# Slots-first relu and two-head turn of q, three output tiles side by side, first denominators by halves

## The chip, the core and the metric

The kernel runs on one core of one Trainium2 chip. The metric is the device time of one execution in microseconds (us), the median of several executions. All executions told of here are of the fast state (granted TensorE clock 0.997 to 1.0), apart from four single looks at the kernel before. The kernel before took 325.89 us (median of 6 runs, 325.66 to 326.36).

## The reference, cut to what matters

Linear attention with a cosine feature map (8 batches, 8 heads, 576 positions, head size 64) feeds a gated feed-forward block (4608 tokens, 512 wide, 1536 hidden). Only relu is applied to q before it is weighted with cosine and sine of the position.

```python
def phi(x, c, s):
    r = np.maximum(x, 0.0)
    return np.concatenate([r * c, r * s], axis=-1)
q_p, k_p = phi(q, cos_w, sin_w), phi(k, cos_w, sin_w)
kv  = np.einsum('bhsf,bhsd->bhfd', k_p, v);   z = np.sum(k_p, axis=2)
den = np.einsum('bhsf,bhf->bhs', q_p, z)[..., None] + 1e-06
x   = np.einsum('bhsf,bhfd->bhsd', q_p, kv) / den      # -> [4608, 512]
...
g   = x @ w_gate
out = (g * (1.0 / (1.0 + np.exp(-g))) * (x @ w_val)) @ w_out
```

## The kernel before

The work goes by groups of 512 tokens. For each group TensorE makes twelve blocks f=0 to 11 of gate and value products (L503, with `wg_sb` and `wv_sb`), ScalarE the silu `sg`, VectorE the product `ht`, and TensorE then the output products with `wo_sb` (L539). While the first group runs, the attention for the next batch has to be made ready in between: q is turned (transposed) by TensorE so that positions become columns, kv is summed up, and the products of the two (the a-products) follow.

The turn before the change reads q as it was loaded. It transposes one head at a time into half of the partitions, and relu is applied as the result is copied out of PSUM (on ScalarE 0.914 us for 128x896 in this kernel):

```python
def qturn_pe(b, j, lo, hi, eng):
    ps = take(1).bitcast(BF16).rearrange("p (c x) -> p c x", x=P)
    for c in range(lo, hi):
        for i in range(2):
            nc.tensor.transpose(out=ps[i * D:(i + 1) * D, c - lo], in_=raws[b, "q"][:, 2 * j + i, c],
                                identity=ident)
    relu_op(eng, qt_of(b)[:, :, j, lo:hi].rearrange("p e c s -> p c e s"),
            ps[:, 0:hi - lo].rearrange("p c (e s) -> p c e s", e=2))
```

Such turns come three times: one slot of q of batch one during block 9, seven slots of batch two after block 11 ("the large turn"), and the last two slots of batch two during the output products ("the second turn"). The order of the start and of blocks 0 to 5 (the first 28.75 us) is written out as a list of words, executed one by one; blocks 6 to 11 run by halves of 256 columns; the output tiles of the first group run two side by side:

```python
words = """
    cq0@act cq1@act tq0 qr0@dve qw0.0 qw0.1 rk1.0@act rk0.0@dve z8 kv0.0 rk3.0@dve rk2.0@dve kv1.0
    ...
""".split()                       # cq cast q, tq turn q, qr relu, qw weight, rk relu k, kv products, z filler products of zeros
...
for g, s in enumerate(("a10", "a11", "b8", "b9")):
    at(s, lambda g=g: vmul(1, g))                 # the four v products on VectorE
at("b11", q_(1, 0, 0), q_(1, 1, 0), lambda: kv_mm(1), lambda: kv_out(1))
...
for nm, f in order:                               # halves a6 a7 b6 b7 a8 ...
    ffn_fc(0, f, *((HALF, GH) if nm == "b" else (0, HALF)))
    slot(f"{nm}{f}")
steps0 = [(piece, t) for piece in range(3) for t in range(2)] + [(piece, t) for t in (2, 3) for piece in range(3)]
for i, (piece, t) in enumerate(steps0):
    ffn_out(t, 4 * piece, 4 * piece + 4)          # a third of wo for one tile of 128 tokens
    slot(divmod(i, 4))
```

## Time and profile before

| stretch of TensorE's stream (profiled run, 326.35 us) | from | to | us |
|---|---|---|---|
| start, until the first gate product | 0 | 16.41 | 16.41 |
| blocks 0 to 5 | 16.41 | 28.75 | 12.34 |
| blocks 6 to 11 | 28.75 | 39.66 | 10.91 |
| large turn, kv, output products, second turn | 39.66 | 55.49 | 15.83 |
| second group to the last product | 55.49 | 320.51 | 265.03 |

Two of these stretches as the view by stretches of time has them. Its columns are the length, then the busy us (and instructions) of TensorE, its weight loads, VectorE, ScalarE and GpSimd, then the granted clock, and two figures for the DMAs (share and GB/s) that are not used here:

```profile
28.75:39.66 10.91, 10.91 (x103) 9.34 (x100) 8.15 (x19) 4.97 (x15) 5.19 (x7) 1.00 1.30 204
39.66:55.49 15.83, 15.83 (x194) 9.12 (x194) 10.28 (x29) 10.23 (x21) 0.00 (x0) 1.00 1.22 222
```

TensorE is busy for the whole of both. The timeline of TensorE around the large turn (start, length, what ran; an idle time would stand in brackets at the end) shows that nothing is waited for there:

```profile
39.13 0.60 PE L503 MATMUL banks<-xT,wv_sb 128*128 128x256 bf16 x4
39.66 0.97 PE L264 MATMUL banks<-ident,raw_q 128*64 128x128 bf16 x28
40.56 1.24 PE L276 MATMUL banks<-v,raw_k 64*64 64x130 bf16 x72
```

The reader should see `128*64` against `128*128`: a turn to half of the partitions is listed with another shape than the products around it. Four products of 256 columns start 0.437 us apart as a block, so the transposes could have begun at 39.57 and began at 39.66: 0.09 us pass at this change of shape.

### The profile page before, as it was taken

What the parts mean: (1) busy time and instruction counts of PE and PEld (TensorE: products, weight loads), DVE (VectorE), ACT (ScalarE), POOL (GpSimd) and SP (SyncE); (2) the same over time, 40 slices, a digit from 0 to 9 for tenths busy, and PEclk for the clock granted to TensorE, in tenths of its full rate; (3) what the DMA queues carried; (4) which work ended last, traced back from release to release, by engine and by line L of the source; (5) the groups of instructions that cost most, each with busy time, mean ns of one, the idle gap of its engine ahead of it and who ended that gap; (6) DMA issues with size and microseconds to landing.
All of it is one profiled execution on the core that took longest, in us unless ns stands there. A gap on an engine that the chain in (4) does not pass through costs nothing.

```text
span 324.6 us, 6212 instructions
## 1 busy us (share of the span) xinstructions
PE 318.0 (98%) x2474; PEld 164.6 (51%) x2474; DVE 181.8 (56%) x366; ACT 132.3 (41%) x247; POOL 34.8 (11%) x58
## 2 busy tenths in 40 slices
PE   7999999999999999999999999999999999999995
PEld 3589855454545444544454445444554445444443
DVE  7775866976575647565657555755564236423420
ACT  7553565943653335332642354344432132213311
POOL 6755200002002000110002000200000000000000
PEclk9999999999999999999999999999999999999999
DMA  7999999499676997699689969794921411240014
GB/s 264 215 199 199 205 205 221 70 125 149 147 125 80 185 153 128 93 170 163 120 111 140 164 129 130 119 186 110 134 46 34 106 26 32 44 103 17 2 32 97
DMA packets 71660, 40.37 MB, mean 124 GB/s; under 512 B 47184, under 2 KB 66384, under 8 KB 71632
## 3 DMA queue, kind: packets, MB, share of 16 engines
q1 hardware_dynamic: 49280, 22.29, 37.9%
q0 software_dynamic: 22192, 17.57, 35.5%
q8 instruction: 19, 0.31, 0.4%
q10 hardware_dynamic: 160, 0.13, 0.1%
q14 instruction: 9, 0.07, 0.1%
HBM read 37.75 MB, written 9.44 MB: 145 GB/s over the span
## 4 chain that ended last, share of the span: by engine, by line
PE 95%; DMA 2%; DVE 1%; ACT 0%; SPq 0%; issue 0%; ACTq 0%
PE banks L503 58%; PE banks L539 28%; PE banks L276 3%; PE banks L390 2%; DMA first_q<-in_q_dram 2%; PE banks L475 1%; PE banks L434 1%; PE banks L149 1%; PE banks L558 1%; PE banks L264 0%; PE banks L316 0%; PE banks L372 0%; SPq L117 0%; DVE qwT L360 0%; ACT ob L561 0%; ACT qf L339 0%
## 5 line engine op out<-in xcount | busy, mean ns | idle before, releaser
L514 DVE TENSOR_TENSOR ht<-sg,banks 128x512 bf16<-128x512 bf16 (+2 forms) x122 | 75.8, 625 | 68.1 <-PE banks L503 62.3
L509 ACT ACTIVATE sg<-banks 128x512 bf16<-128x512 f32 (+2 forms) x122 | 66.9, 548 | 113.6 <-PE banks L503 109.0
L503 PE MATMUL banks<-xT,wv_sb 128*128 128x512 bf16 (+2 forms) x488 | 112.8, 355 | 0.1
L503 PE MATMUL banks<-xT,wg_sb 128*128 128x512 bf16 (+2 forms) x488 | 112.6, 355 | 0.0
L539 PE MATMUL banks<-wo_sb,ht 128*128 128x512 bf16 x420 | 94.3, 379 | 0.0
L503 PEld LDWEIGHTS <-wv_sb 128*128 128x128 bf16 x488 | 47.2, 98 | 46.7 <-issue 0.4
L503 PEld LDWEIGHTS <-wg_sb 128*128 128x128 bf16 x488 | 45.7, 98 | 41.6
L539 PEld LDWEIGHTS <-ht 128*128 128x128 bf16 x420 | 40.1, 98 | 45.2 <-issue 0.2
L546 ACT COPY ob<-banks 128x512 f32<-128x512 f32 x18 | 10.5, 585 | 51.2 <-PE banks L539 49.2
L232 DVE TENSOR_TENSOR r_q<-raw_q,tab 128x1152 bf16<-128x1152 bf16 x24 | 17.9, 754 | 20.2 <-ACT raw_q L215 20.2
L546 DVE COPY ob<-banks 128x512 f32<-128x512 f32 x17 | 11.8, 691 | 28.9 <-PE banks L539 28.0
L236 DVE TENSOR_TENSOR v<-raw_v,tab 128x1152 bf16<-128x1152 bf16 x31 | 23.0, 752 | 0.3 <-ACT raw_v L570 0.3
L411 DVE TENSOR_TENSOR x<-banks,rec 128x512 bf16<-128x512 f32 (+1 forms) x32 | 21.5, 674 | 1.1
L714 POOL COPY hold<-phit 1x2 bf16<-1x2 bf16 x5 | 0.9, 176 | 155.1 <-DMA phit<-r_q 155.1
L215 ACT ACTIVATE raw_q<-raw_q 128x576 bf16<-128x576 bf16 x24 | 15.7, 680 | 0.8 <-DMA raw_q<-in_q_dram 0.8
L215 ACT ACTIVATE raw_k<-raw_k 128x576 bf16<-128x576 bf16 x24 | 16.0, 675 | 0.0
L390 PEld LDWEIGHTS <-phit 128*128 128x128 bf16 (+1 forms) x240 | 9.9, 100 | 6.0 <-issue 1.3
L390 PE MATMUL banks<-kv,phit 128*128 128x65 bf16 (+1 forms) x240 | 11.5, 195 | 0.0
L149 PE MATMUL banks<-zeros 128*128 128x64 bf16 (+1 forms) x66 | 8.7, 290 | 1.0 <-DVE zeros L144 1.0
L299 DVE CAST kv<-banks 64x260 bf16<-64x260 f32 x12 | 5.1, 428 | 7.4 <-ACT kv L299 7.4
L276 PEld LDWEIGHTS <-raw_k 64*64 64x64 bf16 x504 | 7.5, 106 | 2.6 <-issue 2.1
L276 PE MATMUL banks<-v,raw_k 64*64 64x130 bf16 x504 | 8.7, 218 | 0.0
(79 smaller groups left out, 134.3 us busy)
## 6 DMA issues: line engine op xcount, KB each, us to landing
out_dram<-ob SPq DMA_DIRECT2D x70, 128.0 KB, 2.4
raw_k<-in_k_dram POOLq DMA_DIRECT2D x7, 576.0 KB, 9.6
raw_q<-in_q_dram POOLq DMA_DIRECT2D x6, 576.0 KB, 6.1
raw_v<-in_v_dram POOLq DMA_DIRECT2D x6, 576.0 KB, 12.3
wo_sb<-in_moe_w_out_dram POOLq DMA_DIRECT2D x3, 512.0 KB, 12.7
wg_sb<-in_moe_w_gate_dram POOLq DMA_DIRECT2D x5, 256.0 KB, 9.0
wv_sb<-in_moe_w_val_dram POOLq DMA_DIRECT2D x5, 256.0 KB, 9.2
wo_sb<-in_v_dram SPq DMA_DIRECT2D x2, 576.0 KB, 4.1
```

The costliest lines, as they stand in the source:

```text
L149: nc.tensor.matmul(out=ps, lhsT=zeros, rhs=zeros[:, 0:cols].unsqueeze(1).to_broadcast([P, 4, cols]), start=True, stop=True)
L215: nc.scalar.activation(out=out, in_=in_, func=AF.Relu)
L232: nc.vector.tensor_tensor(out=st[b, "q"][:, g], in0=o.unsqueeze(2).to_broadcast([P, NC, 2, D]), in1=tab, op=ALU.mult)
L236: nc.vector.tensor_tensor(out=v2s[b % 2][:, g, :, :, 0:D], in0=(first if b == 0 and g == 0 else {"v": raw_of(b, "v")})["v"][:, g].unsqueez ...
L276: nc.tensor.matmul(out=ps[i * D:(i + 1) * D, e, j * 2 * D1:(j + 1) * 2 * D1], lhsT=raws[b, "k"][es, g, c], rhs=v2s[b % 2][es, g, c, :, 0:D ...
L390: nc.tensor.matmul(out=ps[ms, e, g * D1:(g + 1) * D1], lhsT=phit[b][:, e, g, c:c + n].rearrange("p c s -> p (c s)"), rhs=kv2s[b % 2][:, e, ...
L411: nc.vector.tensor_tensor(out=st["x", t].rearrange("p (y e d) -> p e y d", e=2, d=D)[:, :, ys], in0=ps[:, :, 0:2 * J * D1].rearrange("p e ...
L503: nc.tensor.matmul(out=st["f", tg, fc, lo][i], lhsT=(wg_sb, wv_sb)[i][:, kc, fs], rhs=xT[tg][:, ts, kc], start=(kc == 0), stop=(kc == KC - 1))
L509: nc.scalar.activation(out=sg[:, 0:n], in_=st["f", tg, fc, lo][0], func=AF.Silu)
L514: nc.vector.tensor_tensor(out=hts[tg % 2][:, fc, r:r + n], in0=st.pop(("s", tg, fc, lo))[:, 0:n], in1=ps[1], op=ALU.mult)
L539: nc.tensor.matmul(out=o_ps[t], lhsT=hts[tg % 2][:, fc, r:r + P], rhs=wo_sb[:, fc], start=(fc == 0), stop=(fc == FC - 1))
L546: (nc.scalar.copy if t % 2 == 0 else nc.vector.tensor_copy)(out=ob, in_=ps)
```

## The change

The intent has four parts. The first denominators are made by halves, with a new list of words for the start and blocks 0 to 5, so that the first group starts earlier. Blocks 6 to 11 run in 512 columns and not by halves. q is put slots-first by a relu on VectorE into a new tile, so that two heads stand side by side and one transpose turns both; the copy out of PSUM is then plain. And three output tiles of the first group run side by side, which puts off the need for the later thirds of wo. The diff, cut to its core:

```diff
+    def relu_slots(b, lo, hi):
+        if "qp" not in st:
+            both = rel.tile([P, G, NC, 2, D], BF16, name="r_q").rearrange("p g c w d -> p (g c w d)")
+            st["qp"] = both.rearrange("p (b c j x) -> p b c j x", b=2, c=NC, j=J)
+        relu_op("dve", st["qp"][:, b, lo:hi].rearrange("p c j (i d) -> p c (j i) d", i=2),
+                raws[b, "q"][:, :, lo:hi].rearrange("p g c d -> p c g d"))
...
         for c in range(lo, hi):
-            for i in range(2):
-                nc.tensor.transpose(out=ps[i * D:(i + 1) * D, c - lo], in_=raws[b, "q"][:, 2 * j + i, c],
-                                    identity=ident)
-        relu_op(eng, qt_of(b)[:, :, j, lo:hi].rearrange("p e c s -> p c e s"),
+            nc.tensor.transpose(out=ps[:, c - lo], in_=st["qp"][:, b, c, j], identity=ident)
+        copy_op(eng, qt_of(b)[:, :, j, lo:hi].rearrange("p e c s -> p c e s"),
...
-        cq0@act cq1@act tq0 qr0@dve qw0.0 qw0.1 rk1.0@act rk0.0@dve z8 kv0.0 rk3.0@dve rk2.0@dve kv1.0
+        cq1@act cq0@dve tq0 qr0@dve rk0.0@act rk1.0@dve qw0.0 qw0.1 z6 kv0.0 rk2.0@dve rk3.0@dve kv1.0
...
+    at("a8", lambda: relu_slots(0, NC - 1, NC))
...
-    at("a9", lambda: relu_k(1, 2, 4, "dve"))
+    at("a9", lambda: relu_k(1, 2, 4, "act"))
-    for g, s in enumerate(("a10", "a11", "b8", "b9")):
+    for g, s in enumerate(("b9", "b9", "b10", "b10")):
         at(s, lambda g=g: vmul(1, g))
+        if g == 2:
+            at(s, lambda: relu_slots(1, 0, CUT))
...
+    at((0, 3), lambda: relu_slots(1, CUT, NC))
...
-    for nm, f in order:
-        ffn_fc(0, f, *((HALF, GH) if nm == "b" else (0, HALF)))
-        slot(f"{nm}{f}")
+    for f in range(6, FC):
+        ffn_fc(0, f)
...
-    steps0 = [(piece, t) for piece in range(3) for t in range(2)] + [(piece, t) for t in (2, 3) for piece in range(3)]
+    steps0 = [(piece, t) for piece in range(3) for t in range(3)] + [(piece, 3) for piece in range(3)]
```

Also in it: one relu of k moves from VectorE to ScalarE and the v products come later in VectorE's order (both in the cut above), `x_den` and `x_rec` take halves, the pools of x and `sg` get one buffer more each, and the choice of a PSUM bank avoids splitting a free pair.

More of the change, by code (lines that the diff above doesn't have):

```diff
@@ L50 @@
     phip = ctx.enter_context(tc.tile_pool(name="phip", bufs=2))
-    xp = ctx.enter_context(tc.tile_pool(name="xp", bufs=3))
+    xp = ctx.enter_context(tc.tile_pool(name="xp", bufs=4))
     xtp = ctx.enter_context(tc.tile_pool(name="xtp", bufs=3))
     smp = ctx.enter_context(tc.tile_pool(name="smp", bufs=3))
-    sgp = ctx.enter_context(tc.tile_pool(name="sgp", bufs=4))
+    sgp = ctx.enter_context(tc.tile_pool(name="sgp", bufs=5))
     obp = ctx.enter_context(tc.tile_pool(name="obp", bufs=4))
@@ L66, in take @@
     def take(n, hold=None):
-        free = [b for b in range(0, 8, n) if not any(b <= x < b + n for r in held.values() for x in r)]
-        b0 = min(free, key=lambda b: sorted(used[b:b + n], reverse=True))
+        taken = {x for r in held.values() for x in r}
+        free = [b for b in range(0, 8, n) if not any(b <= x < b + n for x in taken)]
+        b0 = min(free, key=lambda b: (n == 1 and hold is not None and hold[0] == "o" and b ^ 1 not in taken,
+                                      sorted(used[b:b + n], reverse=True)))
         if hold is not None:
@@ L395, in a_tile2, with x_den, x_rec @@
         x_of(t, ps)
-    def x_den(t, ps):
-        den = smp.tile([P, H, 1], FP32, name="den")
+    def x_den(t, ps, ys=slice(0, 4)):
+        if ys.start == 0:
+            st["den", t] = smp.tile([P, H, 1], FP32, name="den")
         nc.vector.tensor_single_scalar(
-            out=den.rearrange("p (e y) o -> p e y o", e=2),
-            in_=ps[:, :, 0:2 * J * D1].rearrange("p e (y x) -> p e y x", x=D1)[:, :, :, D:D1], scalar=1e-6, op=ALU.add)
-        st["den", t] = den
-    def x_rec(t):
-        rec = smp.tile([P, H, 1], FP32, name="rec")
-        nc.vector.reciprocal(out=rec, in_=st.pop(("den", t)))
-        st["rec", t] = rec
-        st["x", t] = xp.tile([P, d_model], BF16, name="x")
+            out=st["den", t].rearrange("p (e y) o -> p e y o", e=2)[:, :, ys],
+            in_=ps[:, :, 0:2 * J * D1].rearrange("p e (y x) -> p e y x", x=D1)[:, :, ys, D:D1], scalar=1e-6, op=ALU.add)
+    def x_rec(t, ps, ys=slice(0, 4)):
+        if ys.start == 0:
+            st["rec", t] = smp.tile([P, H, 1], FP32, name="rec")
+            st["x", t] = xp.tile([P, d_model], BF16, name="x")
+        nc.vector.reciprocal(out=st["rec", t].rearrange("p (e y) o -> p e y o", e=2)[:, :, ys],
+                             in_=st["den", t].rearrange("p (e y) o -> p e y o", e=2)[:, :, ys])
     def x_mul(t, ps, ys=slice(0, 4)):
@@ L418, in x_of @@
         x_den(t, ps)
-        x_rec(t)
+        x_rec(t, ps)
         x_mul(t, ps)
@@ L620 @@
     words = """
-        cq0@act cq1@act tq0 qr0@dve qw0.0 qw0.1 rk1.0@act rk0.0@dve z8 kv0.0 rk3.0@dve rk2.0@dve kv1.0
-        kvo00@act rk3.1@dve kvo01@act rk2.1@dve kv1.1 tq1 kvo10@act kvo11@dve a0.0 qr1@dve a0.1 qw1.0 tq3
-        qw1.1 tq2 den0 qr3@act rec0 x0.0 a1.0 a1.1 qr2@act x0.1 xt0.0 qw3.1 xt0.1 xc0.0@act qw3.0 xc0.1@act
-        den1 z2 a3.0 rec1 G1.0 x1.0 a3.1 s1.0 G0.0 V0.0 qw2.0 s0.0 xt1.0 qw2.1 V1.0 xc1.0@dve a2.0 a2.1 m1.0
-        G1.1 den3 den2 V1.1 rec3 s1.1 G2.01 x3.0 G3.01 s2.01 m1.1 V2.01 rec2 s3.01 x2.0 xt3.0 V3.01
-        xc3.0@act m2.01 xt2.0 m3.01 G5.01 xc2.0@dve G4.01 s5.01 m0.0 G0.23 s4.01 V0.23 s0.23 G1.23 m0.23
-        G5.23 s1.23 V1.23 s5.23 V4.01 m1.23 V5.23 m4.01 V5.01 m5.23 G2.23 m5.01 V2.23 s2.23 G3.23 m2.23
-        V3.23 s3.23 G4.23 m3.23 V4.23 s4.23 G0.1 m4.23 V0.1 s0.1 m0.1
+        cq1@act cq0@dve tq0 qr0@dve rk0.0@act rk1.0@dve qw0.0 qw0.1 z6 kv0.0 rk2.0@dve rk3.0@dve kv1.0
+        kvo01@act rk3.1@dve kvo00@act rk2.1@dve kv1.1 a0.0 kvo11@act kvo10@dve tq1 den0.0 rec0.0 a0.1 x0.0
+        qr1@act tq2 den0.1 rec0.1 qw1.1 tq3 qr2@act qw1.0 xt0.0 x0.1 a1.0 qr3@act a1.1 qw2.0 xt0.1 qw2.1
+        xc0.0@act den1 z2 a2.0 rec1 xc0.1@act a2.1 x1.0 G1.0 G0.0 qw3.1 s1.0 xt1.0 s0.0 qw3.0 V0.0 xc1.0@act
+        V1.0 den2 rec2 a3.0 x2.0 a3.1 G0.1 G1.1 den3 s0.1 V1.1 rec3 s1.1 xt2.0 x3.0 G2.01 xc2.0@act V0.1
+        m1.0 V2.01 s2.01 m0.0 m0.1 xt3.0 m1.1 G3.01 m2.01 xc3.0@act V3.01 s3.01 G1.23 m3.01 V1.23 s1.23
+        G0.23 m1.23 V0.23 s0.23 G5.23 m0.23 G4.01 s5.23 G2.23 s4.01 G4.23 s2.23 G5.01 s4.23 V5.01 s5.01
+        V5.23 m5.01 G3.23 m5.23 V3.23 s3.23 V4.23 m3.23 V2.23 m4.23 V4.01 m2.23 m4.01
     """.split()
@@ L634 @@
         whole, a, part = b not in ("0", "1") or a != "0", int(a), int(b or 0)
+        ys = slice(0, 4) if whole else slice(2 * part, 2 * part + 2)
         if op == "z":
@@ L653 @@
         elif op == "den":
-            x_den(a, st["a", a])
+            x_den(a, st["a", a], ys)
         elif op == "rec":
-            x_rec(a)
+            x_rec(a, st["a", a], ys)
         elif op == "x":
-            x_mul(a, st["a", a], slice(0, 4) if whole else slice(2 * part, 2 * part + 2))
+            x_mul(a, st["a", a], ys)
             st["a", a, "n"] = st.get(("a", a, "n"), 0) + 1
@@ L674 @@
                 ffn_mul(0, a, *span)
-    order = []
-    for f in range(6, FC, 2):
-        order += [("a", g) for g in (f, f + 1)]
-        order += [("b", g) for g in (f, f + 1)]
     def turn_last():
@@ L699 @@
     at((2, 0), turn(6, True))
+    at((0, 3), lambda: relu_slots(1, CUT, NC))
     at((2, 1), q_(1, 0, 1), q_(1, 1, 1))
     at((2, 2), turn(7, True))
-    HALF = GH // 2
-    for nm, f in order:
-        ffn_fc(0, f, *((HALF, GH) if nm == "b" else (0, HALF)))
-        slot(f"{nm}{f}")
-    steps0 = [(piece, t) for piece in range(3) for t in range(2)] + [(piece, t) for t in (2, 3) for piece in range(3)]
+    for f in range(6, FC):
+        ffn_fc(0, f)
+        slot(f"a{f}")
+        slot(f"b{f}")
+    steps0 = [(piece, t) for piece in range(3) for t in range(3)] + [(piece, 3) for piece in range(3)]
     for i, (piece, t) in enumerate(steps0):
```

## The prediction

> **What bounds the kernel now.** I read the page first, then the chain of waits in order of time, then the timeline of each engine in the stretches that the diff touches, then the landings of the DMAs. The chain first, by line and then piece by piece:
>
> ```profile
> PE 95%; DMA 2%; DVE 1%; ACT 0%; SPq 0%; issue 0%; ACTq 0%
> ...
> 12.78 0.43 DVE kvd L324
> 13.21 0.34 DVE qr L217
> 13.55 0.02 issue
> 13.58 0.76 DVE qwT L360 x2
> 14.34 0.09 DVE den L399
> 14.43 0.02 issue
> 14.45 0.21 DVE rec L406
> 14.66 0.02 issue
> 14.69 0.44 DVE x L411
> ...
> 35.90 0.23 PE banks L264 x4
> 36.13 3.60 PE banks L503 x32
> 39.73 0.90 PE banks L264 x28
> 40.63 1.17 PE banks L276 x67
> 41.81 0.97 PE banks L539 x4
> ```
>
> From 15.17 us to 319.78 us the chain is TensorE alone; only the first 15 us belong to DMA, ACT and VectorE. So from there on a change pays only by what it takes off TensorE's own stream or its waits. To see how much is there I took start-to-start spacings: four 256-column matmuls start 0.437 us apart as a block (33.12 to 33.55 in TensorE's timeline), 109 ns each; 512 columns take 216 ns (40 in 8.63 us); 128 columns 56 ns. From 16.41 (first gate product) to 28.75 (first product of block f=6) are 12.34 us, and the stream explains 32 x 55.7 ns + 80 x 109.2 ns + 12 a-products x 57.5 + 12 transposes x 55.7 = 11.88. The 0.46 us left are waits: 0.20 at 19.80 and 0.20 at 23.94, both a value product waiting for the silu of its own gate half, and 0.06 at 17.87. From 28.75 to the end there is no wait at all, only 0.09 us at each change of matmul shape. Everything from the second FFN group (55.49 us) on is the same code in both kernels and stays saturated: it moves as a block.
>
> Two other queues run close behind. The DMA stream lands in a fixed order and is not touched by the change: k of batch one's last part 11.30, q of batch two (seven slots) 37.76, first third of wo 40.29, second 42.84, third 45.92, last q slots 46.30. And VectorE before the q turn:
>
> ```profile
> 34.07 0.45 DVE L217 TENSOR_SCALAR raw_k<-raw_k 128x1152 bf16<-128x1152 bf16 x1
> ...
> 37.90 0.75 DVE L236 TENSOR_TENSOR v<-raw_v,tab 128x1152 bf16<-128x1152 bf16 x1
> 38.57 0.41 DVE L514 TENSOR_TENSOR ht<-sg,banks 128x256 bf16<-128x256 bf16 x1
> 38.90 0.75 DVE L236 TENSOR_TENSOR v<-raw_v,tab 128x1152 bf16<-128x1152 bf16 x1
> 39.57 0.41 DVE L514 TENSOR_TENSOR ht<-sg,banks 128x256 bf16<-128x256 bf16 x1
> ```
>
> It runs without a gap here, but in the kernel before TensorE's transposes at 39.66 read q straight from the load (landed 37.76) and need none of it.
>
> [...] 1152 elements took 0.75 us two-source (1152/1.92 = 600 ns plus 0.15) and 0.45 us one-source (300 ns plus 0.15). [...] The trace has 0.09 us at each change. [...]
>
> **The change part by part.**
> (1) Fewer, wider products. Blocks f=6 to 11 go from 96 products of 256 columns to 48 of 512: 96 x 109.2 = 10.48 us becomes 48 x 215.8 = 10.36, saving 0.12. [...]
> (2) q turned two heads at a time: 40 transposes to 128x64 tiles become 20 to 128x128. The old ones start in pairs 56 ns apart, the new ones singly, so the transposes themselves save nothing; the shape changes do. Turn of the last slot of batch one: 0.33 us (35.74 to 36.06) becomes 2 x 56 = 0.11, saving 0.22. Turn of two slots at 53.18: 0.44 becomes 4 x 56 = 0.22, saving 0.22. The large turn: 0.03 (a change into the kv products stays). Together 0.47.
> (3) The start. With one q cast on VectorE, TensorE's first transposes end 0.3 us earlier; one k relu goes ahead of the q weights, so the first kv products start near 10.33 (ACT's relu, 9.53 to 10.21, plus the 0.12 us that the trace shows) and not 11.00. But the last k part lands at 11.30 and needs two VectorE operations of 0.3 us: kv ends at 12.3 and not 12.70. Then the a-products of the first half go ahead of the q turns, and their denominators with them: kv copy 12.38, den 12.73, rec 12.92, then x must wait for the other half's products (end 13.34), x at 13.38 and not 14.69. This is undone in part: VectorE still has the same operations to do, and x1 (692 ns) starts at 16.14 and not 16.455. Walking row by row with the measured lengths (q weights 0.33 apart, den 0.19, rec 0.24 to the next) the first gate product starts at 16.33 against 16.41, with 24 of 32 a-products done and not 20. After it I find waits of 0.11 for x1, 0.20 for a silu and 0.04 at a copy, 0.35 against 0.46. Sum: 0.08 + 4 x 57.5 ns + 0.11 = 0.42, so f=6 starts at 28.33. With (1) and the first half of (2) TensorE is through f=11 at 28.33 + 10.36 + 0.11 = 38.80 and not 39.57: 0.77 ahead.
> (4) What is added: VectorE must now relu q into the new layout before any transpose, and I see it placed between the third and the fourth v product, after the ht product of f=10. Counted from f=6's start F: ht of f=9 at F+7.18 (the value products end at F+7.07; 0.61 to the next), two v products of 0.67 each, so ht of f=10 cannot start before F+9.12; then 0.61, v 0.67, and the relu starts at F+10.4. Its destination is one run of 1792, its source 7 x 4 x 64: [...] 1792/1.92 = 933 + 150 ns = 1.08 us (estimate from [...] the 0.75 us row). The transposes then start at F+11.54 = 39.87, 0.2 us later than before, and TensorE stands idle about 1.07 us ahead of them. The gain of (1) to (3) up to there is eaten. At 39.87 q has landed long ago, and kv, its copies and the a-products follow with the same distances as before, so piece 0 of wo starts near 41.9, after its landing at 40.29.
> (5) Three output tiles side by side: as many products; it moves the need for the second and third part of wo later (43.5 and more against 42.84; 48 and more against 45.92). The kernel before had no wait there either: worth 0. The small relu of the last q slots (512 elements, 0.28 us) sits in VectorE's slack ahead of turns that had 0.38 us and more to spare.
> Sum: +0.21 at the large turn, -0.03 in it, -0.22 in the second turn = -0.04 us. No gain worth the name.
>
> **The rivals.** (a) The relu [...]: 0.62 us, TensorE's idle is 0.6, and the time falls by 0.5 to 325.4. For: the 0.45 us row[...]. (b) The start gains more than I count, say 1 us, because the half denominators let x0 be ready 1.3 us earlier; then 325.0. Against: q weights, den, rec and x keep VectorE busy through to x1, and every transpose wait is on x. The wait in (4) is counted from F, so such a gain passes on. (c) The DMA stream becomes the bound: TensorE 1.4 us ahead would meet wo at 40.29. By (4) it can't get there. (d) VectorE loses more: one k relu of 1152 took 0.65 us and not 0.45; if the q relu and its neighbours stretch like that, +0.3 to +0.6, 326.4. (e) The silus and copies that now wait for other banks bring new stalls in the first group; I traced each wait of TensorE to its releaser and found each done by then, but 0.2 us either way is easily missed.
>
> **Range and chances.** -0.04 by the sum, and rivals (a) and (b) weigh more than (d) and (e): I say 325.7, with 324.9 (b in full) to 326.5 (d) for eight in ten. 2% is 6.5 us; the parts of the stream that the change touches hold under 2 us of waits in all, and the rest is unchanged, so same 0.97.
>
> **What would show it right or wrong.** Right: first transpose of the large turn near 39.9 with about 1 us idle before it, released by VectorE's relu of q; that relu at 1.0 to 1.1 us; f=6's first product near 28.3; the second FFN group starting within 0.3 us of 55.49; the stretch from there to the end equal to 0.1 us. Wrong if the relu takes 0.6 us (a), if f=6 starts before 27.9 (b) or after 28.8, if TensorE waits on a DMA near 40 (c), or if a wait appears after the second group starts, which I hold to be unchanged.

The 1.92 and the 150 ns of step (4) come from two rows of the trace of before: VectorE's two-source products took 0.419 us for 512 elements (`qwT`) and 0.752 for 1152 (`v`), so 1.92 elements a ns and 0.15 us fixed. With the same 0.15, the one-source row of 0.453 us for 1152 ran at 3.8 elements a ns. That the relu of q would go at the slower of the two paces was my estimate; the trace of before does not show it.

## The result, and the profile after

The changed kernel is correct and took 326.09 us (median of 6 runs, 325.84 to 326.29), against 325.89 before. The ratio is 1.0003, with a 95% interval of 0.999 to 1.0016: the same. Ratios here and below are the mean time of one kernel's fast runs over that of the other's of the same rounds, so they are not quite the ratio of the medians. Every timed run below counts as "same" at 2%; what is told apart lies far under that.

The line of busy times on the page shows TensorE with 70 instructions fewer (2474 before) and the same share; it stays the bound:

```profile
PE 317.7 (98%) x2404; PEld 160.3 (49%) x2404; DVE 181.3 (56%) x362; ACT 133.5 (41%) x244; POOL 34.9 (11%) x58
```

The same two stretches in the changed kernel, by its own marks (first product of block 6, first transpose of the large turn, first product of the second group):

```profile
27.99:39.51 11.52, 10.63 (x52) 4.71 (x50) 7.63 (x15) 4.86 (x9) 5.32 (x8) 1.00 1.32 203
39.51:55.08 15.58, 15.58 (x174) 9.15 (x175) 11.02 (x30) 9.86 (x20) 0.00 (x0) 1.00 1.22 218
```

Blocks 6 to 11 have become 0.61 us longer although TensorE's work in them has become less: 10.63 busy of 11.52. The second stretch is 0.25 shorter. TensorE's timeline shows where the idle time is and what ended it:

```profile
37.59 1.03 PE L513 MATMUL banks<-xT,wv_sb 128*128 128x512 bf16 x4
39.51 0.95 PE L274 MATMUL banks<-ident,r_q 128*128 128x128 bf16 x14 [0.89 <-DVE r_q L220]
40.39 1.24 PE L285 MATMUL banks<-v,raw_k 64*64 64x130 bf16 x72
```

The transposes, half as many and now of shape `128*128`, waited for VectorE's relu of q. (0.89 is counted from the modelled end of the products; by the spacing of starts, the transposes came 1.05 us later than the stream would have let them.) On VectorE, in its timeline, the relu stands behind other work in a row without a gap:

```profile
37.10 0.68 DVE L524 TENSOR_TENSOR ht<-sg,banks 128x512 bf16<-128x512 bf16 x1
37.70 0.75 DVE L239 TENSOR_TENSOR v<-raw_v,tab 128x1152 bf16<-128x1152 bf16 x1
38.37 1.08 DVE L220 TENSOR_SCALAR r_q<-raw_q 128x1792 bf16<-128x1792 bf16 x1
39.37 0.75 DVE L239 TENSOR_TENSOR v<-raw_v,tab 128x1152 bf16<-128x1152 bf16 x1
```

The chain of waits says the same: VectorE was 1% of it before, and now

```profile
PE 94%; DVE 3%; ACT 1%; issue 0%; ACTq 0%
...
20.28 14.78 PE banks L513 x104
...
35.18 0.67 DVE ht L524
35.85 1.11 DVE v L239 x2
...
37.10 0.68 DVE ht L524
37.79 0.67 DVE v L239
38.46 1.00 DVE r_q L220
...
39.51 0.95 PE banks L274 x14
```

From 35.18 to 39.46 the chain runs through VectorE, where in the kernel before it never left TensorE. From the second group to the last product both kernels take 265.03 us.

**A tool for the rest: f=6 (block 6) as a clock.** In the two kernels and in the variants below, the start of block 6 was read from each profiled run together with that run's time. For the six profiled runs of the kernel before, time minus start of block 6 was 297.60, 297.62, 297.60, 297.59, 297.60 and 297.63, while the times themselves ran from 325.76 to 326.35. So practically all of the scatter of this kernel lies before block 6, and what comes after it can be compared to a few hundredths of a us, far finer than the times allow. The table has all profiled runs, in us. "q" is the landing of the first load of q; "to turn" is block 6 to the large turn; "to group 2" is the turn to the second group's first product.

| run | q | block 6 | to turn | to group 2 | the last two together |
|---|---|---|---|---|---|
| before (the profile above) | 7.99 | 28.750 | 10.912 | 15.823 | 26.735 |
| before_again | 7.74 | 28.494 | 10.913 | 15.821 | 26.734 |
| before_look | 7.50 | 28.487 | 10.913 | 15.819 | 26.732 |
| before_look_2 | 7.15 | 28.392 | 10.913 | 15.820 | 26.733 |
| before_look_3 | 6.96 | 28.156 | 10.913 | 15.819 | 26.732 |
| before_look_4 | 7.82 | 28.721 | 10.913 | 15.818 | 26.731 |
| after | 6.98 | 27.987 | 11.521 | 15.576 | 27.097 |
| after_old_start | 8.03 | 28.790 | 11.522 | 15.575 | 27.097 |
| relu_even | 7.20 | 28.044 | 11.061 | 15.574 | 26.635 |
| start_only | 7.95 | 28.108 | 10.912 | 15.906 | 26.818 |
| raw_all | 8.04 | 28.169 | 10.793 | 15.821 | 26.614 |
| raw_turn | 7.01 | 27.961 | 10.565 | 15.592 | 26.157 |
| raw_turn_2 | 7.41 | 28.205 | 10.565 | 15.592 | 26.157 |
| raw_turn_two_tiles | 7.75 | 28.129 | 10.565 | 15.593 | 26.158 |

### The profile page after: what moved, and what is told of

Read it like the earlier page. It is cut to its first block, busy times and chain, and to the rows that moved or that the text cites. A ratio compares the mean times of both kernels' runs of the same rounds, so it can differ in the third digit from the quotient of the medians.

```text
span 324.2 us, 6058 instructions
## 1 busy us (share of the span) xinstructions
PE 317.7 (98%) x2404; PEld 160.3 (49%) x2404; DVE 181.3 (56%) x362; ACT 133.5 (41%) x244; POOL 34.9 (11%) x58
## 4 chain that ended last, share of the span: by engine, by line
PE 94%; DVE 3%; ACT 1%; issue 0%; ACTq 0%
PE banks L513 57%; PE banks L549 28%; PE banks L285 3%; PE banks L399 2%; DVE v L239 1%; PE banks L485 1%; PE banks L444 1%; PE banks L381 1%; PE banks L152 1%; PE banks L568 1%; PE banks L325 0%; DVE ht L524 0%; PE banks L274 0%; ACT L184 0%; DVE r_q L220 0%
## 5 line engine op out<-in xcount | busy, mean ns | idle before, releaser
L524 DVE TENSOR_TENSOR ht<-sg,banks 128x512 bf16<-128x512 bf16 (+2 forms) x116 | 74.8, 650 | 69.5 <-PE banks L513 62.8
L519 ACT ACTIVATE sg<-banks 128x512 bf16<-128x512 f32 (+2 forms) x116 | 65.8, 568 | 111.8 <-PE banks L513 107.6
L513 PE MATMUL banks<-xT,wv_sb 128*128 128x512 bf16 (+2 forms) x464 | 111.3, 364 | 0.0
L513 PE MATMUL banks<-xT,wg_sb 128*128 128x512 bf16 (+2 forms) x464 | 111.3, 364 | 0.0
L513 PEld LDWEIGHTS <-wv_sb 128*128 128x128 bf16 x464 | 44.9, 98 | 48.7
L513 PEld LDWEIGHTS <-wg_sb 128*128 128x128 bf16 x464 | 43.4, 98 | 43.3
L556 DVE COPY ob<-banks 128x512 f32<-128x512 f32 x17 | 11.7, 691 | 28.3 <-PE banks L549 27.4
L218 ACT ACTIVATE raw_k<-raw_k 128x576 bf16<-128x576 bf16 (+1 forms) x25 | 17.2, 695 | 0.0
L152 PE MATMUL banks<-zeros 128*128 128x64 bf16 (+1 forms) x64 | 9.4, 310 | 1.0 <-DVE zeros L147 1.0
```

The costliest lines, as they stand in the source:

```text
L152: nc.tensor.matmul(out=ps, lhsT=zeros, rhs=zeros[:, 0:cols].unsqueeze(1).to_broadcast([P, 4, cols]), start=True, stop=True)
L218: nc.scalar.activation(out=out, in_=in_, func=AF.Relu)
L513: nc.tensor.matmul(out=st["f", tg, fc, lo][i], lhsT=(wg_sb, wv_sb)[i][:, kc, fs], rhs=xT[tg][:, ts, kc], start=(kc == 0), stop=(kc == KC - 1))
L519: nc.scalar.activation(out=sg[:, 0:n], in_=st["f", tg, fc, lo][0], func=AF.Silu)
L524: nc.vector.tensor_tensor(out=hts[tg % 2][:, fc, r:r + n], in0=st.pop(("s", tg, fc, lo))[:, 0:n], in1=ps[1], op=ALU.mult)
L556: (nc.scalar.copy if t % 2 == 0 else nc.vector.tensor_copy)(out=ob, in_=ps)
```

## The experiments

Two theories stood at first. **Theory V**, that of the prediction: VectorE's relu of q, put ahead of the large turn and taking 1.08 us, eats what the other parts save. **Theory L**, the rival formed after the first look at the result: the new start saves little, because the first loads land at another time in every run, and the profile of before happened to have a late landing. All twelve runs gave correct results.

### before_again: the kernel before, unchanged, timed like the others

The edit: none.

> The kernel before, unchanged, for a second trace. Its first profile fell on its slowest run (326.36 us, span 324.6) and had the first q landing at 7.99 us; the changed kernel's had it at 6.98 with nothing changed in that load. Theory L (the landing of the first loads varies from run to run, whatever the kernel): this trace has the first q anywhere from 7.0 to 8.0 us, and if early, the first product of block f=6 starts at 27.9 to 28.3 us instead of 28.75 and the span is 324.1. Rival (the changed kernel makes its loads land early): q at 8.0 and f=6 at 28.75 again. Time 325.9 both ways, ratio 1.000.

Measured: 326.11 us (325.72 to 326.41, 5 runs), ratio 1.0004 (0.9992 to 1.0017). The method shows no difference where there is none, and half a us is at its limit. Block 6 started 0.256 us earlier than in the first profile, with q landed 0.25 earlier.

### start_only: the new start, everything else as before

```diff
--- before
-        cq0@act cq1@act tq0 qr0@dve ...
+        cq1@act cq0@dve tq0 qr0@dve ...
+    (x_den and x_rec by halves, one buffer more for x and for sg)
```

> The new start alone (word order, half denominators, two pools one deeper), everything else as before. My prediction's step 3 counted 0.42 us for it with late loads: 325.5, ratio 0.9987. Under theory L it gains that only when the loads are late; with early loads its q cast on VectorE waits for the v products anyway (8.07 us), and it is within 0.2 us of before: 325.8, ratio 0.9995 to 1.0. In the trace the large turn's transposes must follow block f=11 without idle time either way.

Measured: 325.76 us (325.70 to 325.91), ratio 0.9995 (0.9982 to 1.0007). That is nearer to theory L's 325.8 than to step 3's 325.5. But block 6 started at 28.108, and the trace shows 0.09 us that neither theory had: with TensorE this early and the output tiles still two by two, it came to the last third of wo before that had landed. It landed at 45.751, the product that needs it began at 45.793, and by the spacing of the products before it should have begun at 45.705. TensorE's timeline:

```profile
44.62 1.03 PE L540 MATMUL banks<-wo_sb,ht 128*128 128x512 bf16 x4
45.48 0.39 PE L435 MATMUL banks<-kvd,phit 128*128 128x260 bf16 x2
45.79 1.02 PE L540 MATMUL banks<-wo_sb,ht 128*128 128x512 bf16 x4
```

Two a-products take 0.22 us (44.40 to 44.62 just before); here 0.31 pass.

### relu_even: the same relu, written so that both outermost counts are even

```diff
--- after
-        relu_op("dve", st["qp"][:, b, lo:hi].rearrange("p c j (i d) -> p c (j i) d", i=2),
-                raws[b, "q"][:, :, lo:hi].rearrange("p g c d -> p c g d"))
+        relu_op("dve", st["qp"][:, b, lo:hi].rearrange("p c j (i d) -> p (j i) c d", i=2),
+                raws[b, "q"][:, :, lo:hi])
```

> The changed kernel with the q relu walked head pair by head pair (outermost dimension 4 on both sides) in place of slot by slot (1792 in one run against 7 x 4 x 64). Parity theory: [...] 1792/3.84 + 0.15 = 0.62 us instead of 1.08, TensorE's idle before the large turn falls from 1.05 to 0.59, the time by 0.46 us: 325.6, ratio to before 0.9993. Rival (strides of the source, not parity, [...]): relu 1.08, idle 1.05, time as the changed kernel, 326.1.

Measured: 325.75 us (325.57 to 326.03), ratio 0.9997 (0.9983 to 1.0011). VectorE's timeline has the same 1792 elements per partition, read 4 x 7 x 64 and not 7 x 4 x 64, in 0.62 us instead of 1.08:

```profile
38.43 0.62 DVE L220 TENSOR_SCALAR r_q<-raw_q 128x1792 bf16<-128x1792 bf16 x1
```

TensorE's wait fell with it, from 1.05 to 0.59, and block 6 to the turn from 11.521 to 11.061: 0.46, all of what the relu became shorter. The expected 325.6 was missed by 0.15 in the median, within the scatter of the start (the five runs span 0.46). The edit changes the strides of the source along with the counts, but the changed kernel itself sets the strides aside: its relu of the last q slots has the same code and the same strides with 2 slots in place of 7, and took 0.28 us for 512 elements, the pace of 0.62 for 1792 (the changed kernel's bf16 relus of q and k in SBUF, 0.219 us for 256, 0.285 for 512 and 0.453 for 1152, give 3.8 elements a ns and 0.15 us of fixed cost, and with these 1792 would take 0.62; an estimate from those three):

```profile
48.53 0.28 DVE L220 TENSOR_SCALAR r_q<-raw_q 128x512 bf16<-128x512 bf16 x1
```

The slow pace was seen at 7 slots alone; the row of 256 is this relu with one slot. Other counts were not run.

### raw_turn: the large turn undone, all else of the change kept

```diff
--- after
+    def qturn_raw(b, j, lo, hi, eng):      # the old body: transposes from raws, relu on the way out of PSUM
+        ...
-        return lambda: qturn_pe(b, j, lo, hi, eng)
+        return lambda: (qturn_pe if part else qturn_raw)(b, j, lo, hi, eng)
...
-        if g == 2:
-            at(s, lambda: relu_slots(1, 0, CUT))
```

> The changed kernel with the large q turn alone put back (raw q transposed head by head, relu on the way out of PSUM); the small turns stay new. If VectorE's relu ahead of the turn is what eats the gain: no idle before the large turn, its first transpose at 38.5 to 38.6 us, the second group at 54.1 to 54.2, time lower by 0.9 to 1.0 than the changed kernel: 325.1, ratio to before 0.998. Rival (the DMA stream is the bound behind it): TensorE then waits at the first output piece for wo, which lands at 40.3 to 40.5, and less than 0.5 us is gained: 325.6 or more.

Measured: 325.11 us (324.96 to 325.56), ratio 0.9977 (0.9965 to 0.999), as expected. Without the relu ahead of it, TensorE's timeline has the 28 old transposes again, directly behind the products:

```profile
37.57 1.03 PE L522 MATMUL banks<-xT,wv_sb 128*128 128x512 bf16 x4
38.53 0.97 PE L282 MATMUL banks<-ident,raw_q 128*64 128x128 bf16 x28
39.43 1.25 PE L294 MATMUL banks<-v,raw_k 64*64 64x130 bf16 x72
```

Theory V is confirmed: with the relu the stretch is 11.521 and without it 10.565, so 0.96 us on the path (the wait of 1.05 less the shape change of 0.09 that now lies in it). Here q had landed 0.98 us before the turn began (37.55). In the changed kernel it landed at 37.99 and the turn was due at 38.46: in the 0.47 us between, a relu of 1.08 does not fit, wherever it stands in VectorE's order. By that, its place behind a v product cost at most 0.38 of the 1.05 (it began at 38.37); this is an estimate that was not run. This version is faster than the kernel before (the interval lies below 1), and 0.94 us shorter than the changed kernel from block 6 to the second group (26.157 against 27.097); against that one it was not timed in the same rounds.

### raw_turn_2: the same kernel once more, beside the next ones

The edit: that of raw_turn.

> raw_turn again, beside the others: 325.1, 0.998 of before, no wait on wo after the turn.

Measured: 325.23 us (325.04 to 325.38), ratio 0.9974 (0.996 to 0.9987). It was run at another time. The gain holds, and both intervals lie below 1.

### raw_turn_two_tiles: raw_turn with the old order of the output tiles

```diff
--- raw_turn
-    steps0 = [(piece, t) for piece in range(3) for t in range(3)] + [(piece, 3) for piece in range(3)]
+    steps0 = [(piece, t) for piece in range(3) for t in range(2)] + [(piece, t) for t in (2, 3) for piece in range(3)]
```

> As raw_turn, but group one's output tiles in the old order, two side by side. In raw_turn TensorE reaches the first wo product at 40.6 us. In the old order it then needs the second third of wo about 2.4 us later (43.0) and the last about 4.6 us later (45.2); those landed at 42.6 to 43.2 and at 45.2 to 45.9 in the runs so far. Theory W (the third tile side by side is worth nothing in the changed kernel only because TensorE is late there, and is needed as soon as it is early): waits of 0.1 to 0.7 us on wo in all, second FFN group 0.1 to 0.7 later than raw_turn's distance from the turn (15.59 us), time 325.2 to 325.8. Rival N (worth nothing at all): no wait on wo, the same 15.6 us, and raw_turn's time of the same rounds, near 325.1.

Measured: 325.2 us (325.04 to 325.89), ratio 0.9979 (0.9967 to 0.9992); turn to second group 15.593 against 15.592. Theory W, as I put it, fell: no wait. The need came 0.2 us later than I had set it, since block 6 of this run began 0.17 later than raw_turn's (28.129 against 27.961). In this run the last third of wo landed at 45.23 and was first used at 45.38:

```profile
45.16 0.39 PE L453 MATMUL banks<-kvd,phit 128*128 128x260 bf16 x2
45.38 1.03 PE L558 MATMUL banks<-wo_sb,ht 128*128 128x512 bf16 x4
```

So 0.15 us were to spare. That landing lay between 45.17 and 45.99 over the runs, and start_only shows 0.09 us of waiting on it. So the third tile side by side is an insurance. Of the two profiled runs with the new start and the old order of tiles one waited 0.09 us and one did not; what it is worth in timed runs is not shown (means 325.37 here, 325.21 for raw_turn_2).

### after_old_start: the change with the old list of words

```diff
--- after
-        cq1@act cq0@dve tq0 qr0@dve ...
+        cq0@act cq1@act tq0 qr0@dve ...
```

> The changed kernel with the old list of the first 16 us (old order of casts, relus and denominators), the rest changed. Step 3 of the prediction (the start gains 0.42, and the relu's wait is counted from f=6, so the gain passes through): f=6 starts at 28.5 to 28.75, 39.9 to 40.3 for the large turn, idle still 1.0 to 1.1, time 0.4 above the changed kernel, 326.5. Theory L (the start gains that only where the first loads land late; by medians of timed runs it is worth 0.2 or so): 326.3. If the start is worth nothing: 326.1.

Measured: 326.02 us (325.88 to 326.72), ratio 1.0004 (0.9991 to 1.0016). The trace is what step 3 said, with block 6 at 28.79 and the turn at 40.31 (0.04 and 0.01 beyond the ranges), TensorE 1.05 us idle before it, so the wait is counted from block 6 and is the same under either start.

```profile
39.17 1.08 DVE L220 TENSOR_SCALAR r_q<-raw_q 128x1792 bf16<-128x1792 bf16 x1
```

The time is not: 326.5 was expected and the median agrees with "the start is worth nothing". The profiled run was the slowest of the five (326.72). With an old start whose runs span 0.84 us, five times can't settle 0.4.

### before_look, before_look_2, before_look_3, before_look_4: the kernel before, for its first loads

The edit: none, four times.

> The kernel before, unchanged, looked at for where its first loads land. Theory L: f=6 moves about one for one with the landing of the first q (7.74 gave 28.49, 7.99 gave 28.75), so a landing near 7.0 would give f=6 near 27.8 to 28.1 and the new start would be worth nothing there; a landing near 7.7 to 8.0 gives 28.5 to 28.75 again. Rival: with an early landing f=6 stays near 28.4 because a later load bounds.

> The kernel before again, for where its first loads land and when f=6 starts. So far 7.50 gave 28.487, 7.74 28.494, 7.99 28.75. Theory L (early landing brings the old start level with the new one, 28.0 to 28.2): any landing at 7.3 or earlier should give f=6 below 28.3. Rival F (a floor at 28.48 or so for the old start): 28.48 also at 7.0 to 7.3.

> As before_look_2: theory L below 28.3 for a landing at 7.3 or earlier; rival F 28.48; a landing after 7.75 moves f=6 one for one under both.

> As before_look_2: theory L below 28.3 for a landing at 7.3 or earlier; rival F 28.48; a landing after 7.75 moves f=6 one for one under both.

Measured: q landed at 7.50, 7.15, 6.96 and 7.82, and block 6 started at 28.487, 28.392, 28.156 and 28.721. Neither theory holds as put: 7.15 gave 28.39 and not below 28.3 (against L), 6.96 gave 28.16 (against the floor F). The old start does follow the landing, by about 0.6 us for one of landing (28.156 to 28.750 for 6.96 to 7.99). The traces show two things that break the one-for-one. In the first three looks TensorE was still in its products of zeros (filler that the kernel issues) when q was cast. Of before_look_2, first ScalarE's timeline, then TensorE's:

```profile
7.17 0.71 ACT L339 CAST qf<-first_q 128x256 bf16<-128x256 f32 x2
```

```profile
6.26 2.28 PE L149 MATMUL banks<-zeros 128*128 128x64 bf16 x41
8.38 0.39 PE L347 MATMUL banks<-ident,qf 128*128 128x128 bf16 x4
```

The cast ended at 7.89, the transposes of q began at 8.38, when the zeros ahead of them in the stream were through. The second thing is that instructions of VectorE took longer beside GpSimd's issues of loads. The new start moves with that (0.31 to 0.56 us for one and the same cast); its lines are shown below, where rival (d) of the prediction is taken up.

### raw_all: nothing slots-first at all

```diff
--- raw_turn
-        return lambda: (qturn_pe if part else qturn_raw)(b, j, lo, hi, eng)
+        return lambda: qturn_raw(b, j, lo, hi, eng)
...
-            qturn_pe(0, j, NC - 1, NC, "act")
+            qturn_raw(0, j, NC - 1, NC, "act")
...
-    at("a8", lambda: relu_slots(0, NC - 1, NC))
...
-    at((0, 3), lambda: relu_slots(1, CUT, NC))
```

> raw_turn with the two small q turns also undone, so that nothing of the slots-first q is left: the new start, the wide products and the three side-by-side tiles alone. Step 2 of the prediction (the two-head turn saves 0.22 at the last slot and 0.22 at the last two slots, by shape changes): from f=6 to the large turn 0.22 longer than in raw_turn (10.57 becomes 10.79), from the turn to the second FFN group 0.22 longer (15.59 becomes 15.81), time 0.4 above raw_turn, 325.6 of 326.1. Rival: shape changes are hidden, then 325.2 as raw_turn.

Measured: 325.67 us (325.64 to 325.83), ratio 0.999 (0.9976 to 1.0004): 0.44 above raw_turn_2's median in another job. Block 6 to the turn 10.793, turn to second group 15.821, both within about 0.01 of what was expected. The reason is in TensorE's timeline around the last-slot turn; first raw_all, then raw_turn:

```profile
35.17 0.30 PE L282 MATMUL banks<-ident,raw_q 128*64 128x128 bf16 x4
35.40 1.04 PE L522 MATMUL banks<-xT,wg_sb 128*128 128x512 bf16 x4
```

```profile
34.87 0.28 PE L274 MATMUL banks<-ident,r_q 128*128 128x128 bf16 x2
34.98 1.03 PE L522 MATMUL banks<-xT,wg_sb 128*128 128x512 bf16 x4
```

From the turn to the next product 0.23 us pass with the old shape and 0.11 with the new one. Before the turn the old shape loses another 0.09, by the spacing of starts.

## Why the prediction was right, point by point

The predicted time was 325.7 (range 324.9 to 326.5), measured 326.09, and "same" was given 0.97. The sum was small because large terms cancel, so it is the terms that have to be checked.

1. **Wider products**, step (1), predicted 0.12 saved. Right: raw_all against before, 10.912 to 10.793, so 0.119. (raw_all has other edits too, but in neither kernel did TensorE wait in this stretch.)
2. **Two heads at a time**, step (2), predicted 0.22 at the last slot, 0.22 at the second turn, 0.03 in the large turn. Right: raw_all to raw_turn 0.228 and 0.229; raw_turn to after 0.016 within the large turn (15.592 to 15.576). The gain comes from the shape changes (0.093 to 0.096 us for each around the turns of q) and not from the smaller number of transposes (14 fewer in the large turn, for the 0.016).
3. **The start**, step (3), predicted 0.42 saved and block 6 at 28.33. In the profiles the difference is as predicted: the six looks at the kernel before have block 6 at 28.50 on average, the seven profiled runs with the new start at 28.09, so 0.41. The larger part of it is fixed, for the reasons given: 24 of the 32 a-products came before the first gate product, and from there to block 6 TensorE took 12.33 to 12.34 us in all seven profiled runs with the old list of words and 11.96 in all seven with the new, 0.38 less (0.34 predicted). What lies before the first gate product moves from run to run, and there the step had no term for the longer cast that is shown below. The timed runs give less than 0.42. If time minus block 6 is 297.60, corrected for each kernel by the last column of the table, then 38 fast runs of the kernel before have block 6 at 28.43 in the mean and 36 runs with the new start at 28.20. This estimate, 0.23 us with a standard error of 0.05, comes out between 0.17 and 0.25 in each of the four sets of rounds: by the timed runs the term was nearly twice too large, and the 0.41 of the profiles may in part be luck of which runs were profiled. The absolute 28.33 was wrong by 0.34 for the changed kernel. One profile's landings (7.99 for q, 11.30 for the last part of k, against 6.98 and 10.30) can be only a part of that, since start_only, with 7.95 and 11.20, began block 6 at 28.11.
4. **The relu ahead of the large turn**, step (4), predicted 1.08 us, starting 10.4 after block 6, transposes 11.54 after it, TensorE idle 1.07. Measured 1.079, 10.38 (38.37 less 27.99), 11.52 and 1.05. Right in each. What the runs show of the pace is 1.079 us for 1792 elements with 7 slots outermost in the source, 0.62 for as many with 4 outermost on both sides (relu_even), and 0.28 for 512 with 2 slots; why the first is slower is not shown.
5. **Side-by-side tiles**, step (5), predicted 0. Right in the changed kernel. The step said that before had no wait there, and there were 0.43 us to spare (45.92 to 46.35); with the earlier start the margin is small (0.15 us in raw_turn_two_tiles, overdrawn by 0.09 in start_only).

The sum from block 6 to the second group: -0.119 - 0.228 - 0.229 + 1.050 - 0.094 (the shape change that now lies in the wait) - 0.016 = +0.364, measured 27.097 less 26.735, so +0.362. With 0.41 from the start this gives -0.05 (predicted -0.04), with the 0.23 of the timed runs +0.13. The medians say +0.2, with an interval of the ratio from -0.3 to +0.5 us, which holds both. Of the signs that the prediction named, one failed: the second group started at 55.08, 0.4 before 55.49 and not within 0.3 of it, because block 6 came earlier than forecast.

Of the rivals, (a) is what relu_even made true on purpose, 0.46 of the 0.5 it named. (b), a start that gains 1 us, and (c), the DMA stream as the bound, did not happen, although start_only touched wo for 0.09. (e), new waits on banks in the first group, did not either: in the changed kernel the waits between the first gate product and block 6 were 0.12 for x and 0.18 for a silu (predicted 0.11 and 0.20).

(d) did not touch the q relu, but it had noticed something real. A k relu had taken 0.65 us and not 0.45 (34.94 to 35.59), and I could not say why; the trace has GpSimd issuing a load from 34.59 to 35.33. The same stretching is what sets the new start, and step (3) has no term for it. In the chain of waits of the kernel before, the load of q comes first:

```profile
1.75 6.24 DMA first_q<-in_q_dram
7.99 0.02 issue
8.01 0.72 ACT qf L339 x2
```

The changed kernel's chain has no load at that place, but VectorE:

```profile
6.06 2.09 DVE v L239 x3
8.16 0.27 DVE qf L348
8.42 0.05 issue
8.47 0.40 PE banks L356 x4
```

that is, the half of q whose cast was moved to VectorE. In all seven profiled runs with the new start this cast began at 8.07 to 8.11, behind the v products, but took between 314 and 560 ns. GpSimd issues the weight loads one after the other at that time, and VectorE's cast ended 116 to 118 ns after the end of such an issue in all seven. A k relu of 128x576 at the start took 0.591 us in the first profile of before and up to 0.817 in others, ending 283 to 285 ns after an issue in the longest cases. That the cast is held up until GpSimd's issue is through is read from these times; by what is not shown. raw_turn, GpSimd's timeline and then VectorE's:

```profile
7.50 0.77 POOL L206 DMA_DIRECT2D wg_sb<-in_moe_w_gate_dram  x1
```

```profile
8.07 0.31 DVE L357 CAST qf<-first_q 128x256 bf16<-128x256 f32 x1
```

and raw_turn_2, where GpSimd was a quarter of a us out of step with that:

```profile
7.73 0.78 POOL L206 DMA_DIRECT2D wg_sb<-in_moe_w_gate_dram  x1
```

```profile
8.07 0.56 DVE L357 CAST qf<-first_q 128x256 bf16<-128x256 f32 x1
```

The issue ended at 8.27 and 8.51, the cast at 8.39 and 8.63. Block 6 came 19.57 to 19.58 us after the end of this cast in six of the seven runs (19.62 in the seventh). So the new start hangs on GpSimd's step and not on the landing of q (read from seven traces; no run moved GpSimd's issues), which is why it moves so little with the landing (27.99 at 6.98, 28.17 at 8.04). It also shows what the new order is worth. From VectorE's relu of the first turned q to block 6 the changed kernel needs 19.08 us (8.904 to 27.987) where the kernel before needs 19.59 (9.157 to 28.750): 0.51 better, of which the later cast gives back about 0.1 in the mean. That a cast on ScalarE in the new order would keep all of the 0.51 is argued from this and was not run.

What stays open: why the part before the first gate product gave back some 0.15 us in the mean of the timed runs (0.38 less 0.23). The longer cast is a candidate, but only profiled runs show it.

## What to carry to other kernels

Work put on another engine to spare the bound engine some instructions pays only if it is done before the bound engine gets there; here a relu of 1.08 us ahead of a turn cost a wait of 1.05 us, to save 0.11 in the turn, while the same relu for the small turns, where VectorE had time, saved 0.46. So such a change should be taken apart by place, and kept where there is slack: keeping all but the large turn gave 325.11 against 325.95 before in the same rounds. And where the scatter between runs lies in one stretch, measure from the end of that stretch: here it told apart hundredths of a us when the times could not tell 0.4.
